# Batch 0 of a fused attention and channel-mix kernel: six loads of k moved to ScalarE's DMA queue and begun ahead

## The chip, the cores and the metric

The kernel runs on one core of a Trainium2 chip. The metric is the device time of one execution in microseconds (us). A profile is one execution with its trace; its span, from the first to the last instruction, is about 1.8 us shorter than the device time of the same execution. Engines: PE is TensorE, DVE is VectorE, ACT is ScalarE, POOL is GpSimd, SP is SyncE, which here only issues DMA. All runs that are compared are fast, apart from one of 743.12 us in the first measurement of the kernel before, which is left out.

## The reference, cut to what matters

```python
def _attn_ref(q, k, v, tau):                       # q, k, v: 4 x 6208 x 256, float32
    qn = q / (norm(q, axis=1) + 1e-06)             # norms over the 6208 rows, one per channel
    kn = k / (norm(k, axis=1) + 1e-06)
    s = kn.transpose(0, 2, 1) @ qn / tau           # 256 x 256 per batch
    a = softmax(s)
    return v @ a
# x = _attn_ref(...); then the channel mix of x: two matmuls with relu squared, gated by a sigmoid
```

For each batch all of q and k must be read before its softmax, and the softmax before the first row of output. For batches 1 to 3 that is hidden behind the mixing of the batch before. For batch 0 nothing can hide it: 12.7 MB (two tensors of 6208 x 256 float32) stand at the start of the kernel.

## The kernel before

Batch 0 is loaded in 14 groups, in the order 1, 2, 0, 3, 4, ... 13. Groups 1 to 11 are 512 rows: one transfer of 512 KB for q and one for k, 128 descriptors of 4 KB each. Group 0 is the 64 left-over rows: 64 descriptors of 1 KB for q, and as many for k. Groups 12 and 13 are half size. Below, "seventh group" means seventh in the order of loading.

```python
    def group_load(b, g):
        rows, n = rows_of(b, g)
        qk = pq.tile([P, S, 2, C], BF16, name="qk", tag="qk", bufs=5)
        groups[b, g] = (qk,)
        if b == 0:
            qk2 = pq.tile([P, S, 2, C], BF16, name="qk2", tag="qk2", bufs=4)
            groups[b, g] += (qk2,)
            t_f = []
            for i, t in enumerate((q, k)):
                f = pq.tile([P, S, C], F32, name=f"f{i}", tag=f"f{i}", bufs=6)
                nc.sync.dma_start(f[:rows, :n], qk_src(t, b, g))
                t_f.append(f)
            groups[b, g] += tuple(t_f)
        # ... (batches 1 to 3 load through GpSimd)

    def group_cast(b, g):
        rows, n = rows_of(b, g)
        qk, qk2, *t_f = groups[b, g]
        for i in range(2):
            nc.vector.tensor_copy(qk[:rows, :n, i, :], t_f[i][:rows, :n])        # to bf16
        for i in range(2):
            nc.scalar.activation(qk2[:rows, :n, i, :], t_f[i][:rows, :n], AF.Square)
    # ...
    nc.scalar.dma_start(mu_rows[0:2], moe_mu_k.rearrange("(h p) -> h p", p=P))   # 1 KB each
    nc.scalar.dma_start(mu_rows[2:4], moe_mu_r.rearrange("(h p) -> h p", p=P))
    # ...
    for g in order(0):
        group_load(0, g)
        group_cast(0, g)
        if g == DIRECT + 1:                     # DIRECT = 9; this is the eleventh group
            copies, gather, roots, evac, invert, turn, exp, weigh = softmax_pieces(0)
            copies()                            # DVE copies the norms' sums out of PSUM
            gather()                            # PE gathers them
        for s in range(sizes(0)[g]):
            unit_matmul(0, g, s)                # s_ps, then PE's sums of the squares (ssq_ps)
        if 5 <= g <= DIRECT:
            keep_warm(3)                        # matmuls that only keep PE busy
    # ... roots, evac, invert, turn (st_ps), exp, weigh: the softmax; then the main pipeline
```

DVE casts, ACT squares, PE multiplies and sums. In the timelines below, ACT's work and the DMA issues of each engine come in the order of the program: in the changed kernel ACT's first square (11.33 us) stands behind its last issue (9.67 us).

## Time and profile before

| kernel before | |
|---|---|
| device time, first measurement | 514.62 and 514.87 us |
| span of the profiled execution | 512.5 us |
| PE busy | 494.6 us (97%) |
| first output-side work (the first `delta` of the mix) | starts at 44.62 us |

The head of the page, its busy rows and its last rows of part 2 (40 slices of 12.8 us; busy share in tenths, then the moved GB/s):

```profile
span 512.5 us, 9496 instructions
PE 494.6 (97%) x3540; PEld 336.7 (66%) x3540; DVE 439.7 (86%) x725; ACT 450.1 (88%) x924; POOL 99.9 (19%) x146
...
PEclk9989999999999999999999999999999999999999
DMA  8999999999989999999599999926498773423123
GB/s 284 410 334 197 198 169 189 148 183 187 207 167 203 185 210 160 163 185 140 96 155 189 186 181 188 186 65 124 83 180 132 114 134 88 101 80 86 44 82 103
```

PE's 97% suggests a kernel that PE bounds, and after the first three slices that is so. But the change touches only those three, and there the moved GB/s are at 410, twice what they are later. The chain that ended last, cut to its longest pieces before 41 us (start, us, what):

```profile
2.18 8.05 DMA f<-in_k_dram
10.26 0.92 ACT qk L144
11.18 9.83 DMA f<-in_k_dram
21.09 10.31 DMA f<-in_k_dram
31.42 0.69 DVE qk L142
32.12 0.61 DVE ssq L225
32.77 1.05 PE bank L232 x8
...
40.37 1.11 PE st_ps L272 x8
```

Until 31.4 us the chain is the loads of q and k. It leaves them at k of the eleventh group (landed at 31.40 us), not at the last group; from there it is PE's work, one piece after the other, to the softmax. The windows view puts the rate of the loads beside it (PE, PEld, DVE, ACT and POOL busy, then the granted clock, the DMA share and GB/s):

```profile
4.00:8.00 4.00, 1.66 (x8) 1.27 (x9) 1.46 (x3) 2.11 (x2) 0.00 (x0) 1.00 0.99 321
8.00:11.00 3.00, 0.99 (x7) 0.21 (x5) 1.44 (x3) 1.80 (x2) 0.00 (x0) 1.00 1.05 283
11.00:31.00 20.00, 17.79 (x113) 8.99 (x113) 10.76 (x17) 16.50 (x18) 0.00 (x0) 1.00 1.02 409
```

From 11 us on the rate is steady at 409 GB/s, one transfer of 512 KB per 1.28 us. From 4 to 11 us it is a quarter lower, though the DMA share says that the engines were occupied (0.99 and 1.05): their packets took longer. SyncE's timeline shows when the loads were issued (start, us it took):

```profile
2.18 0.43 SPq L131 DMA_DIRECT2D f<-in_k_dram  x1
2.65 0.57 SPq L131 DMA_DIRECT2D f<-in_q_dram  x1
3.27 0.59 SPq L131 DMA_DIRECT2D f<-in_k_dram  x1
3.90 0.58 SPq L131 DMA_DIRECT2D f<-in_q_dram  x1
4.52 0.78 SPq L131 DMA_DIRECT2D f<-in_k_dram  x1
5.35 0.65 SPq L131 DMA_DIRECT2D f<-in_q_dram  x1
6.04 0.44 SPq L131 DMA_DIRECT2D f<-in_k_dram  x1
8.18 0.33 SPq L131 DMA_DIRECT2D f<-in_q_dram  x1
10.25 0.33 SPq L131 DMA_DIRECT2D f<-in_k_dram  x1
```

The last two lines are the sixth group. They went out only when the second group's q (8.16 us) and k (10.23 us) had landed: the built program waits so that no more than eight transfers are outstanding.

### The profile page before, as it was taken

The numbers are of one execution on the slowest core, as the hardware profiler recorded it, in microseconds if no ns is written. First come the engines' busy times: TensorE is split into PE (matmuls) and PEld (weight loads), VectorE is DVE, ScalarE is ACT, GpSimd is POOL, SyncE is SP. The second block draws the span as 40 slices with busy tenths as digits, with TensorE's granted clock in tenths as the row PEclk, the third lists the DMA queues.
The fourth block names the chain that finished last, engine by engine and source line by source line (L and its number), as shares of the span: only waits on it lengthen the run. The fifth ranks groups of instructions, "written<-read, shape, count | busy, mean of one in ns | idle before, by whom it ended". The sixth has DMA issues, their size and how long they took to land.

```text
span 512.5 us, 9496 instructions
## 1 busy us (share of the span) xinstructions
PE 494.6 (97%) x3540; PEld 336.7 (66%) x3540; DVE 439.7 (86%) x725; ACT 450.1 (88%) x924; POOL 99.9 (19%) x146
## 2 busy tenths in 40 slices
PE   3889999999999999999999999999999999999996
PEld 1455666776576667667666677677666666666675
DVE  3556899999999999999979999999878787878884
ACT  5886999999899999999899999999887888878784
POOL 0035341223044122121243133000131100000000
PEclk9989999999999999999999999999999999999999
DMA  8999999999989999999599999926498773423123
GB/s 284 410 334 197 198 169 189 148 183 187 207 167 203 185 210 160 163 185 140 96 155 189 186 181 188 186 65 124 83 180 132 114 134 88 101 80 86 44 82 103
DMA packets 133462, 83.46 MB, mean 163 GB/s; under 512 B 50660, under 2 KB 126760, under 8 KB 133416
## 3 DMA queue, kind: packets, MB, share of 16 engines
q0 software_dynamic: 56592, 33.01, 50.0%
q1 hardware_dynamic: 76656, 49.72, 42.9%
q8 instruction: 27, 0.44, 0.3%
q14 instruction: 19, 0.16, 0.1%
q10 hardware_dynamic: 168, 0.13, 0.1%
HBM read 78.71 MB, written 25.43 MB: 203 GB/s over the span
## 4 chain that ended last, share of the span: by engine, by line
PE 85%; DMA 6%; DVE 4%; ACT 4%; issue 1%; SPq 0%; DVEq 0%
PE vr_ps L460 31%; PE kT_ps L423 30%; PE vr_ps L456 8%; PE xT_ps L352 7%; PE s_ps L182 6%; DMA f<-in_k_dram 6%; ACT kr L428 1%; DVE acc L169 1%; DVE xk L408 1%; DVE kk L441 1%; PE st_ps L272 1%; ACT sq L163 1%; ACT xT L354 1%; DVE delta L398 1%; PE junk_ps L513 0%
## 5 line engine op out<-in xcount | busy, mean ns | idle before, releaser
L428 ACT ACTIVATE kr<-kT_ps 128x512 bf16<-128x512 f32 (+1 forms) x392 | 232.7, 605 | 28.9 <-PE kT_ps L423 24.9
L423 PE MATMUL kT_ps<-xk,w_k_sb 128*128 128x512 bf16 (+1 forms) x784 | 231.2, 377 | 0.4 <-DVE xk L408 0.2
L460 PE MATMUL vr_ps<-w_v_sb,kk 128*128 128x256 bf16 x1536 | 231.0, 273 | 0.1
L460 PEld LDWEIGHTS <-kk 128*128 128x128 bf16 x1536 | 149.6, 98 | 58.8 <-DVE kk L441 1.1
L470 DVE SCALAR_TENSOR_TENSOR res<-res,vr_ps 128x256 f32<-128x256 f32 x192 | 79.8, 416 | 44.2 <-ACT res L469 44.1
L441 DVE TENSOR_TENSOR kk<-kr 128x1536 bf16<-128x1536 bf16 (+2 forms) x148 | 116.9, 790 | 0.2 <-ACT kr L428 0.2
L423 PEld LDWEIGHTS <-w_k_sb 128*128 128x128 bf16 x784 | 75.9, 98 | 28.6 <-issue 1.2
L169 DVE TENSOR_TENSOR acc<-acc,sq 128x1024 f32<-128x1024 f32 x69 | 84.0, 1218 | 0.0
L182 PE MATMUL s_ps<-qk 128*128 128x256 bf16 x392 | 73.5, 289 | 6.5 <-DVE qk L142 6.5
L469 ACT ACTIVATE res<-vr_ps 128x256 f32<-128x256 f32 x192 | 76.2, 397 | 1.3 <-PE vr_ps L460 1.3
L456 PE MATMUL vr_ps<-w_r_sb,xr 128*128 128x256 bf16 x384 | 73.3, 272 | 1.2 <-DVE res L470 1.2
L408 DVE SCALAR_TENSOR_TENSOR xk<-delta,mu_t,xT 128x512 bf16<-128x512 bf16 x96 | 71.4, 745 | 0.0
L408 DVE SCALAR_TENSOR_TENSOR xr<-delta,mu_t,xT 128x512 bf16<-128x512 bf16 x96 | 71.3, 745 | 0.0
L456 PEld LDWEIGHTS <-xr 128*128 128x128 bf16 x384 | 37.6, 98 | 46.4 <-issue 2.5
L354 ACT CAST xT<-xT_ps 128x512 bf16<-128x512 f32 x94 | 55.3, 589 | 12.1 <-PE xT_ps L352 12.1
L352 PE MATMUL xT_ps<-vT,a_sb 128*128 128x512 bf16 x188 | 55.9, 379 | 0.2 <-DVE vT L335 0.2
L136 POOL DMA_DIRECT2D qk<-in_q_dram x39 | 26.3, 675 | 143.6 <-ACT kr L428 62.5
L182 PEld LDWEIGHTS <-qk 128*128 128x128 bf16 x392 | 39.4, 103 | 18.1 <-issue 8.1
L165 ACT ACTIVATE sq<-qk 128x1024 f32<-128x1024 bf16 (+1 forms) x49 | 50.8, 1036 | 0.0
L315 POOL DMA_DIRECT2D v_bf<-in_v_dram x48 | 37.4, 782 | 49.6 <-DMA vT<-v_bf 21.3
L398 DVE TENSOR_TENSOR delta<-xT 128x1024 bf16<-128x1024 bf16 x48 | 32.9, 686 | 1.9 <-ACT xT L354 1.8
L144 ACT ACTIVATE qk<-f 128x1024 bf16<-128x1024 f32 (+2 forms) x28 | 26.1, 948 | 8.3 <-DMA f<-in_q_dram 5.3
(82 smaller groups left out, 214.1 us busy)
## 6 DMA issues: line engine op xcount, KB each, us to landing
out_dram<-res SPq DMA_DIRECT2D x47, 512.0 KB, 4.3
v_bf<-in_v_dram POOLq DMA_DIRECT2D x48, 256.0 KB, 9.2
qk<-in_q_dram POOLq DMA_DIRECT2D x36, 256.0 KB, 8.2
qk<-in_k_dram POOLq DMA_DIRECT2D x36, 256.0 KB, 9.2
f<-in_q_dram SPq DMA_DIRECT2D x11, 512.0 KB, 9.0
f<-in_k_dram SPq DMA_DIRECT2D x11, 512.0 KB, 9.9
vT<-v_bf SPq DMA_TRANSPOSE x44, 9.3
f<-in_q_dram SPq DMA_DIRECT2D x2, 256.0 KB, 8.5
```

The costliest lines, as they stand in the source:

```text
L169: nc.vector.tensor_tensor(sums[b], sums[b], t, op=OP.add)
L182: nc.tensor.matmul(s_ps[:, ih, :], rows_at(qk, b, g, 0)[:rows, s, ih * P:(ih + 1) * P], rows_at(qk, b, g, 1)[:rows, s, :], start=t0 and ih ...
L352: nc.tensor.matmul(xT_ps, a_sb[:, b, ih, dh * P:(dh + 1) * P], vT[:, :, ih, :], start=ih == 0, stop=ih == 1)
L354: nc.scalar.copy(xT[:, dh, 1:], xT_ps)
L408: nc.vector.scalar_tensor_tensor(o[:, dh], st[i, "d"][:, dh], mu[:, dh:dh + 1], st[i, "x"][:, dh, :M], op0=OP.mult, op1=OP.add)
L423: nc.tensor.matmul(kT_ps[:, :m], w_k_sb[:, dh, fh * P:(fh + 1) * P], xk[:, dh, :m], start=dh == 0, stop=dh == 1)
L428: nc.scalar.activation(kr, kT_ps[:, :m], AF.Relu, scale=0.5 ** 0.5)
L441: nc.vector.tensor_tensor(st[i, "kk"][:, fh // 4 * 4 + lo:fh + 1, :m], kr, kr, op=OP.mult)
L456: nc.tensor.matmul(vr_ps[:, D:], xr[:, dh, s * P:(s + 1) * P], w_r_sb[:, dh, :], start=dh == 0, stop=dh == 1)
L460: nc.tensor.matmul(vr_ps[:, :D], kk[:, fh, s * P:(s + 1) * P], w_v_sb[:, fh, :], start=fh == 0, stop=fh == 7)
L469: nc.scalar.activation(res[:, s], vr_ps[:, D:], AF.Tanh, scale=0.5)
L470: nc.vector.scalar_tensor_tensor(res[:, s], res[:, s], 1.0, vr_ps[:, :D], op0=OP.add, op1=OP.mult)
```

## The change

The intent is to begin the first six groups at once, k on ScalarE's queue beside q on SyncE's, so that SyncE's issuing doesn't hold back the start. The allocation of the bf16 tiles moves from the load to the cast, so that the loads can stand ahead of everything.

```diff
     def group_load(b, g):
         rows, n = rows_of(b, g)
-        qk = pq.tile([P, S, 2, C], BF16, name="qk", tag="qk", bufs=5)
-        groups[b, g] = (qk,)
         if b == 0:
-            qk2 = pq.tile([P, S, 2, C], BF16, name="qk2", tag="qk2", bufs=4)
-            groups[b, g] += (qk2,)
             t_f = []
             for i, t in enumerate((q, k)):
                 f = pq.tile([P, S, C], F32, name=f"f{i}", tag=f"f{i}", bufs=6)
-                nc.sync.dma_start(f[:rows, :n], qk_src(t, b, g))
+                (nc.scalar if i and order(0).index(g) < 6 else nc.sync).dma_start(f[:rows, :n], qk_src(t, b, g))
                 t_f.append(f)
-            groups[b, g] += tuple(t_f)
+            groups[b, g] = tuple(t_f)
         # ... (batches 1 to 3: the tile is allocated in the else branch)
     def group_cast(b, g):
         rows, n = rows_of(b, g)
-        qk, qk2, *t_f = groups[b, g]
+        t_f = groups[b, g]
+        qk = pq.tile([P, S, 2, C], BF16, name="qk", tag="qk", bufs=5)
+        qk2 = pq.tile([P, S, 2, C], BF16, name="qk2", tag="qk2", bufs=4)
+        groups[b, g] = (qk, qk2)
     # ...
+    for g in order(0)[:6]:
+        group_load(0, g)
     for g in order(0):
-        group_load(0, g)
+        if (0, g) not in groups:
+            group_load(0, g)
         group_cast(0, g)
```

More of the change, by code (lines that the diff above doesn't have):

```diff
@@ L130, in group_load @@
                 f = pq.tile([P, S, C], F32, name=f"f{i}", tag=f"f{i}", bufs=6)
-                nc.sync.dma_start(f[:rows, :n], qk_src(t, b, g))
+                (nc.scalar if i and order(0).index(g) < 6 else nc.sync).dma_start(f[:rows, :n], qk_src(t, b, g))
                 t_f.append(f)
-            groups[b, g] += tuple(t_f)
+            groups[b, g] = tuple(t_f)
         else:
+            qk = pq.tile([P, S, 2, C], BF16, name="qk", tag="qk", bufs=5)
+            groups[b, g] = (qk,)
             for i, t in enumerate((q, k)):
@@ L139, in group_cast @@
         rows, n = rows_of(b, g)
-        qk, qk2, *t_f = groups[b, g]
+        t_f = groups[b, g]
+        qk = pq.tile([P, S, 2, C], BF16, name="qk", tag="qk", bufs=5)
+        qk2 = pq.tile([P, S, 2, C], BF16, name="qk2", tag="qk2", bufs=4)
+        groups[b, g] = (qk, qk2)
         for i in range(2):
```

## The prediction

> **What bounds the kernel now.** The span is 512.5 us; PE is busy 97% of it and makes up 85% of the chain of waits. The change touches only batch 0's q and k, the first 39 us. There the chain is nearly all DMA: "f<-in_k_dram" from 2.18 to 31.42 us, then DVE and PE up to the softmax (st_ps at 40.4 us). The windows view gives 406 to 414 GB/s from 11 to 31 us: transfer-bound, one 512 KB tile per 1.28 us. Before that it is uneven: 407 GB/s at 3 to 4 us, then 254 to 365 GB/s up to 11 us. Against 410 GB/s about 0.75 MB are lost there, an estimated 1.8 us.
>
> The timeline shows why SyncE doesn't issue all at once: an issue takes 0.4 to 0.8 us, and q and k of the sixth group go out only at 8.18 and 10.25 us, as earlier tiles land (at most eight transfers outstanding).
>
> **What the change does.** Six of 28 loads move to ScalarE's queue. Bytes, casts, squares and matmuls are unchanged, as is the built order on PE and DVE. The Trainium skill, "DMA: Bandwidth & Descriptors", section "Issuing engines are not separate DMA queues", says that both queues end on the same 16 DMA engines and only issue time is saved. This trace agrees that issue isn't the limit in the steady part (0.33 us per 1.28 us of transfer). So no higher steady rate; at best part of the 1.8 us comes back.
>
> **What it costs.** In the built order the limit of eight is shared by both queues, and ScalarE executes in order: its six issues stand before its table load (1.28 us) and first square. Its third issue waits for a mu load, the fourth to sixth for landings of q and k of the first group and k of the second. So "all at once" won't happen; the sixth issue goes out when k of the second group lands, which I estimate at 8 to 9.5 us, and the first square starts near 10.2 us instead of 4.12. ScalarE has about 26.4 us of squares (22 at 1.06, four at 0.57, two at 0.4) and took 2.25 of every 2.56 us before: it regains 0.3 to 0.4 us per group. Its backlog of about 4 us should be gone about when the last groups land: squares end at 37 to 38 us (37.3 before). PE's norm matmuls (L197) wait on those squares, so PE idles at 8 to 12 us, then catches up, at half speed until 18 us (8 matmuls 1.87 us, later 1.03). Buffers come free later (seventh q issued at 11.5 us instead of 10.74), but with several tiles still queued; DMA shouldn't starve.
>
> **Sum.** DMA: 0 to -1.5 us. ScalarE/PE backlog at the end of batch 0: 0 to +1. Net about -0.2 us, passed on to the end, because batch 0's softmax gates everything. I predict 514.7 us, 80% range 513.0 to 516.2. Faster by over 2%: 1%; within 2%: 97%; slower: 2%.
>
> **What would show it.** Right: first ACT square at 9 to 11 us; ACT almost without idle from there to 30 us; steady rate near 410 GB/s; last cast of batch 0 at 35 to 37 us; Sqrt within 1.2 us of its 39.08. Wrong: a rate above 420 GB/s, first square before 7 us, or DMA gaps after 11 us because buffers wait for squares.
>
> **What would make it wrong.** The early unevenness may be wholly an effect of the single queue (gain up to 2 us). The late PE may get its full clock one period later than 18 us, or escape or repeat the half-speed stretch at 35 to 38.6 us (about 1 us either way).

## The result, and the profile after

| | before | after |
|---|---|---|
| device time, first comparison | 514.87 us, median of its three fast runs (514.62, 514.87, 516.22) | 513.47 us median (513.42 to 513.62, 4 runs) |
| span of the profiled execution | 512.5 us | 511.8 us |
| Sqrt of the norms starts | 39.08 us | 38.38 us |
| first `delta` starts | 44.62 us | 43.99 us |
| from there to the end | 467.89 us | 467.86 us |

The ratio of the fast runs is 0.9966, with a 95% interval of 0.9945 to 0.9987. A ratio is the mean time of one kernel's fast runs over that of the other's of the same rounds, so it is not quite the ratio of the medians. The change counts as "same" at 2%.

The last two rows say where the difference lies: the part of the kernel after the first `delta` takes the same time in both traces, and the 0.6 to 0.7 us are made before it. The head of the page, its busy row and the GB/s row of its part 2:

```profile
span 511.8 us, 9499 instructions
PE 491.9 (96%) x3540; PEld 336.2 (66%) x3540; DVE 439.6 (86%) x725; ACT 448.2 (88%) x924; POOL 99.9 (20%) x146
...
GB/s 323 409 306 199 196 168 191 163 177 185 214 147 167 204 226 164 162 198 126 101 150 214 151 187 196 181 70 120 83 181 132 97 151 90 100 81 85 43 82 103
```

The traced executions took 514.28 and 513.62 us, 0.66 us apart. The medians are 1.40 us apart, so about half of the timed difference is explained by the traces; the rest belongs to executions that were not traced.

The first slice moves 323 GB/s instead of 284, the second 409 (410 before): the start became faster, the steady rate did not. The same windows of the changed kernel:

```profile
4.00:8.00 4.00, 0.30 (x2) 0.31 (x3) 1.57 (x4) 0.00 (x0) 0.00 (x0) 1.00 1.02 390
8.00:11.00 3.00, 1.80 (x8) 1.03 (x8) 1.61 (x5) 0.96 (x1) 0.00 (x0) 1.00 1.03 355
11.00:31.00 20.00, 16.33 (x118) 8.65 (x117) 10.38 (x17) 19.33 (x23) 0.00 (x0) 1.00 1.03 409
```

ScalarE's timeline of the first 21 us, without its first line, which the prediction was most concerned with:

```profile
1.33 0.24 ACTq L508 DMA_DIRECT2D mu_rows<-in_moe_mu_r_dram  x1
1.60 8.41 ACTq L127 DMA_DIRECT2D f<-in_k_dram  x6
10.04 1.28 ACT L145 ACT_TABLE_LOAD   x1 [10.04 <-DMA f<-in_k_dram]
11.33 10.19 ACT L145 ACTIVATE qk<-f 128x1024 bf16<-128x1024 f32 x12
```

The same two pieces of work in the kernel before:

```profile
1.61 1.28 ACT L144 ACT_TABLE_LOAD   x1 [1.61 <-PEq L696]
4.12 1.06 ACT L144 ACTIVATE qk<-f 128x1024 bf16<-128x1024 f32 x1 [1.23 <-DMA f<-in_q_dram]
```

The loads were not begun at once. ACT's six issues took from 1.60 to 10.01 us, because the last three of them (4.10, 7.19 and 9.67 us) stand until earlier transfers have landed (4.08, 7.17 and 9.65 us). The third waits for a mu load, but that had landed at 2.04 us and cost nothing. The table load and the first square stand behind the issues. The chain of the changed kernel therefore goes through ACT's late start, and leaves it again at 19.65 us (pieces under 0.3 us left out):

```profile
1.99 7.66 DMA f<-in_k_dram
9.67 0.34 ACTq L127
10.04 1.28 ACT L145
...
18.59 1.05 ACT qk L145
19.65 11.13 DMA f<-in_k_dram
30.81 0.69 DVE qk L143
31.50 0.61 DVE ssq L226
32.15 1.05 PE bank L233 x8
...
39.72 1.13 PE st_ps L273 x8
```

From 19.65 us on the chain is one load, from its issue to its landing 11.13 us later. It lay in the queue behind others all that time, while 409 GB/s went on; so the chain's way through ACT up to there doesn't mean that ACT's late start delayed that landing. From k of the eleventh group on the chain is that of the kernel before, 0.6 us sooner at every step (30.78 for 31.40 us, 32.15 for 32.77, 39.72 for 40.37).

In the traces each of these loads ends with 16 reports, one from each DMA engine. So a landing has a middle and a last report, and the work starts after the last: DVE's cast of k of the eleventh group began at 31.42 us, its last report was at 31.40 us. From these records (us):

| landing (last of 16 reports) | before | after | sooner by |
|---|---|---|---|
| k of the first group | 5.80 | 7.17 | -1.37 |
| k of the second group | 10.23 | 9.65 | 0.58 |
| q of the seventh group | 19.74 | 18.01 | 1.73 |
| k of the tenth group | 28.70 | 26.97 | 1.73 |
| q of the eleventh group | 30.11 | 29.50 | 0.61 |
| k of the last group | 36.66 | 36.05 | 0.61 |

Two things happened: 1.73 us were won at the start, and 1.12 us of it were lost between the tenth and the eleventh group. By the middle report 0.99 us were won at q of the seventh group (18.71 to 17.72 us); the rest is a narrower spread between first and last report (1.39 to 0.41 us). The experiments ask what won, and the trace tells what may have lost.

**What lost.** In every trace one packet of 16 KB on the queue that the page calls "instruction" comes between 25.9 and 29.8 us and takes 1.02 to 1.11 us on its engine, against 0.16 us on average for a packet of 4 KB of the loads (11 to 26 us). After the change it starts at 27.02 us and takes 1081 ns; from the transfer then in flight on, the spread between first and last report rises from 0.40 to 1.66 us. Before, it starts at 27.94 us and takes 1079 ns, and the spread rises only from 1.38 to 1.45 us: there five of the 16 reports were 0.6 to 1.0 us behind the middle one already. The middle report of q of the eleventh group was 1.04 us sooner (27.96 against 29.00), the last only 0.61.

Whose instructions are they? In the two traces the packet starts after 221 (before) and 210 (after) PE matmuls and weight loads, and the following ones come at intervals of about 260 of them (484, 749, 991 before). The Trainium skill, "Runtime: NRT & Kernel Launch", section "Instruction fetch mechanics", says that an engine's instructions are refilled in blocks of 16 KiB, 256 instructions, through a DMA queue of the sequencer. That agrees with PE's stream in size and interval. The section calls the cost "mostly hidden", from the side of the engine that is fed. For the loads, which share a DMA engine with the block, it doesn't look hidden here. That the packet causes the lag is read from the coincidence in 13 of the 14 traces (in two of them, before and one_queue, the spread rose by 0.2 us or less), not from a run that moves the packet alone. (In the fourteenth, late_act, the spread was 2.05 us before and after.)

### The profile page after: what moved, and what is told of

Same layout as the page of the kernel before. It is cut to its first block, busy times and chain, and to the rows that moved or that the text cites. A ratio compares the mean times of both kernels' runs of the same rounds, so it can differ in the third digit from the quotient of the medians.

```text
span 511.8 us, 9499 instructions
## 1 busy us (share of the span) xinstructions
PE 491.9 (96%) x3540; PEld 336.2 (66%) x3540; DVE 439.6 (86%) x725; ACT 448.2 (88%) x924; POOL 99.9 (20%) x146
## 4 chain that ended last, share of the span: by engine, by line
PE 86%; ACT 5%; DVE 4%; DMA 4%; issue 1%; ACTq 0%; DVEq 0%
PE vr_ps L461 31%; PE kT_ps L424 30%; PE vr_ps L457 8%; PE xT_ps L353 7%; PE s_ps L183 7%; DMA f<-in_k_dram 4%; ACT kr L429 1%; DVE acc L170 1%; DVE xk L409 1%; DVE kk L442 1%; ACT qk L145 1%; PE st_ps L273 1%; ACT sq L164 1%; ACT xT L355 1%; DVE delta L399 1%
## 5 line engine op out<-in xcount | busy, mean ns | idle before, releaser
L183 PE MATMUL s_ps<-qk 128*128 128x256 bf16 x392 | 71.8, 283 | 3.7 <-DVE qk L143 3.7
L143 DVE CAST qk<-f 128x1024 bf16<-128x1024 f32 (+2 forms) x28 | 17.5, 644 | 14.0 <-DMA f<-in_k_dram 9.4
```

What stands on the lines that cost most here:

```text
L183: nc.tensor.matmul(s_ps[:, ih, :], rows_at(qk, b, g, 0)[:rows, s, ih * P:(ih + 1) * P], rows_at(qk, b, g, 1)[:rows, s, :], start=t0 and ih ...
```

## The experiments

Twelve runs were made, in three groups, each group on one chip and on another chip than the last. A comparison of two times is made only within a group.

**Group 1: is it the queue?** The first trace alone doesn't even show that the slow start belongs to the kernel. So the kernel before was traced again.

before_again: no edit.

> The kernel before, unchanged, profiled a second time. The first trace of it shows three stalls of the loads: eight packets of 0.75 to 1.5 us at 4.6 to 4.9 us, and all packets slowed to 0.3 to 0.5 us at 8.0 to 9.0 and 9.5 to 10.3 us. Theory A (the single queue causes the slow start): they come again, about 250 to 370 GB/s from 4 to 11 us, and k of the sixth group lands near 18.5 us again. Rival B (chance, a disturbance of that one execution): the second trace has other or no stalls, 390 to 410 GB/s from 3 us on, and k of the sixth group lands near 16.5 to 17 us. Ratio to before: 1.000 within 0.003 in both.

Measured: the slow start came again: 323 GB/s from 4 to 8 us and 299 from 8 to 11 us, nine packets over 0.6 us (up to 1.61 us) near 4.6 to 6.0 us. Theory A holds against chance. The time is a warning, though: 513.79 us median (513.60 to 514.30), ratio 0.9973 (0.9957 to 0.9990) to the identical kernel before, whose 11 runs on the same chip lay between 513.56 and 515.93 us. Two identical programs differ by as much as the change gains, with an interval that leaves 1 out. So the time of one pair of programs proves nothing under half a per cent, and the traces have to carry the argument.

one_queue: the change, with all loads on SyncE's queue.

```diff
-                (nc.scalar if i and order(0).index(g) < 6 else nc.sync).dma_start(f[:rows, :n], qk_src(t, b, g))
+                nc.sync.dma_start(f[:rows, :n], qk_src(t, b, g))
```

> The change with all loads on SyncE's queue: only the order of buffer allocation and the up-front loop are left of it. Theory A (the second queue gives the gain): as before, 250 to 370 GB/s from 4 to 11 us, q of the seventh group lands near 19.7 us, ratio 1.000 within 0.001. Rival C (the order of allocation gives it): ratio 0.997, early rate near 390 GB/s.

Measured: 345 and 310 GB/s in the two windows, three packets of 1.37 to 1.48 us at 4.97 to 5.02 us, q of the seventh group at 19.70 us; ratio 1.0002 (0.9986 to 1.0019). The allocation and the loop ahead do nothing that shows; rival C falls. (This trace also has five packets of 0.62 to 0.99 us near 1.8 to 2.5 us. Such early ones come with one queue and with two, in late_act, shallow, after and two_in_order as well, and are not counted here.)

late_act: one_queue, and ACT must first copy one element of the second group's k.

```diff
     for g in order(0)[:6]:
         group_load(0, g)
+    held = const.tile([P, 1], F32, name="held")
+    nc.scalar.copy(held, groups[0, order(0)[1]][1][:, 0, 0:1])
```

> All loads on SyncE's queue, as one_queue, but ScalarE copies one element of the second group's k before its first square, so that its squares start as late as in the changed kernel (about 10 us). Rival D (the early stalls come from ScalarE's table load and squares running beside the first loads, and the change gains by holding ScalarE back): early rate near 390 GB/s, q of the seventh group lands near 18 us, ratio near 0.997. Theory A (queue): early rate as before, 19.7 us, ratio 1.000 to 1.004, because the late squares are then on top of the late loads.

Measured: 347 and 326 GB/s, one packet of 1.30 us at 4.80 us, q of the seventh group at 19.83 us; ratio 0.9993 (0.9977 to 1.0010). The first square began at 10.32 us. So holding ACT back doesn't make the loads faster; rival D falls. It also bounds the price of the late squares: against one_queue, k of the last group landed at the same time (36.51 and 36.52 us), Sqrt came 0.25 us later (39.09 against 38.84), and the matmuls after it (st_ps) only 0.03 us later (40.22 against 40.19). Even the 0.25 us need not be the squares': in both traces the chain from k of the eleventh group on is PE's, and PE's half-clock stretch began 0.42 us sooner in late_act (33.71 against 34.13 us).

two_on_act: only k of the first two groups on ACT's queue, which no landing holds up.

```diff
-                (nc.scalar if i and order(0).index(g) < 6 else nc.sync).dma_start(f[:rows, :n], qk_src(t, b, g))
+                (nc.scalar if i and order(0).index(g) < 2 else nc.sync).dma_start(f[:rows, :n], qk_src(t, b, g))
```

> Only k of the first two groups on ScalarE's queue, which no landing holds up, so that ScalarE's squares start near 4 us as before. Theory A: the early rate is 390 GB/s or more as in the change, q of the seventh group lands near 18 us and ratio 0.995 to 0.998. Rival D (late ScalarE helps): stalls are back, ratio near 1.000. If the queue must stay shared for all six groups, the rate falls back after the second group.

Measured: 371 and 393 GB/s, no packet over 0.6 us before 26 us, q of the seventh group at 17.89 us, first square at 4.02 us; 513.60 us median (513.41 to 513.75), ratio 0.9968 (0.9954 to 0.9983). In these traces two transfers on the second queue bring all that six bring, and ACT isn't held up. Span and Sqrt are as after the change (511.8 us, 38.30 us), which agrees with late squares that cost next to nothing.

**Group 2: what is the slow start made of?** All traces with one queue have two dips: long packets at 4.6 to 5 us, and a general slowness at 8 to 10.5 us, when the 1 KB packets of group 0 pass.

late_left: the kernel before, with group 0 loaded seventh.

```diff
-        return [1, 2, 0] + g[3:]
+        return [1, 2, 3, 4, 5, 6, 0] + g[7:] if b == 0 else [1, 2, 0] + g[3:]
```

> The kernel before (one queue), with the short group 0 (64 rows of 1 KB for q and for k) loaded seventh instead of third. All four traces with one queue have two stalls: single packets of 0.65 to 1.6 us at 4.6 to 5.0 us, and 190 to 290 GB/s at 8 to 10.5 us. Theory E (the second stall belongs to the 1 KB packets of group 0, which pass at 7.5 to 9.5 us): the first stall stays, 8 to 10.5 us runs at 380 GB/s or more, and a smaller dip comes where group 0 now passes (near 16 to 18 us). Rival F (it belongs to the number of transfers issued at the start to one queue): both stalls stay where they were. Time within 0.3% of before in both cases.

Measured: 338 GB/s from 4 to 8 us, with six packets of 0.93 to 1.51 us, but 412 from 8 to 11 us; the spread of the landings rose from 1.15 to 2.12 us where group 0 now passed, near 18 to 21 us. So the second dip belongs to group 0 (theory E), the first doesn't. Time 514.42 us, ratio 0.9989 (0.9970 to 1.0008): the dip is moved, not removed.

shallow: the kernel before, with fewer transfers outstanding at the start.

```diff
                 f = pq.tile([P, S, C], F32, name=f"f{i}", tag=f"f{i}", bufs=6)
+                if 3 <= order(0).index(g) < 6:
+                    nc.vector.memset(f[:, 0, 0:1], 0.0)
 # ... and in the main loop the load of the group three places ahead stands behind the cast
```

> The kernel before (one queue, same order), but the loads of the fourth to sixth group each wait until an earlier group is cast (a one-column write to their buffers), so that at 4.5 us only three large and two small transfers are outstanding on the queue instead of five large and two small. Theory F (issuing many transfers into one queue at the start stalls it): no single packets over 0.6 us near 4.6 to 5.0 us, 380 GB/s or more from 4 to 7 us, and issues of 0.3 to 0.5 us. Rival E (the kind of transfer): the first stall goes or stays by chance, the second stays at 8 to 10.5 us. If neither changes, both fall.

Measured: with nothing issued between 3.85 and 6.34 us there still were four packets of 0.99 to 1.17 us at 4.79 to 4.86 us, and 302 GB/s at 8 to 11 us. So the first dip comes without many issued transfers and without SyncE's issuing at that moment; theory F falls as it was put. The rate from 4 to 8 us was 371 GB/s, though, above the other traces with one queue (321 to 347), so that a deep queue makes the dip worse isn't excluded. (The hold was too long: the fifth group went out at 10.40 us, and the rate was 205 GB/s from 11.5 to 12.0 us. The time, 515.61 us, ratio 1.0016 with 0.9988 to 1.0044, is of no use for that reason.)

two_late_left: two_on_act, with group 0 loaded seventh, the same edit as in late_left.

> k of the first two groups on ScalarE's queue and group 0 loaded seventh. Theory E: the remaining dip of two_on_act (336 to 358 GB/s at 6 to 9 us, where the 1 KB packets passed) goes or moves to near 16 us; q of the eighth group in order lands 0.3 us or more sooner than in two_on_act by the sum of bytes; the time is 0 to 0.4 us under two_on_act (513.6 us). Rival F: no change, 513.6 us.

Measured: 408 GB/s from 4 to 8 us and 419 from 8 to 11 us. The two edits together remove both dips:

| GB/s at 4 to 8 / 8 to 11 us | one queue | two queues |
|---|---|---|
| group 0 third | 321 / 283 (before) | 371 / 393 (two_on_act) |
| group 0 seventh | 338 / 412 (late_left) | 408 / 419 (two_late_left) |

The windows of the two kernels on the diagonal:

```profile
4.00:8.00 4.00, 2.15 (x13) 1.37 (x13) 1.60 (x4) 2.26 (x3) 0.00 (x0) 1.00 1.02 338
8.00:11.00 3.00, 1.59 (x10) 0.88 (x7) 1.81 (x3) 2.53 (x3) 0.00 (x0) 1.00 1.01 412
```

(late_left, above: the first window slow, the second not.)

```profile
4.00:8.00 4.00, 0.23 (x1) 0.28 (x2) 1.50 (x4) 1.80 (x2) 0.00 (x0) 1.00 1.03 371
8.00:11.00 3.00, 2.99 (x16) 1.59 (x16) 2.12 (x5) 2.83 (x5) 0.00 (x0) 1.00 1.02 393
```

(two_on_act: in the first window group 0's small packets pass, and they cost less than with one queue.) And yet the time did not follow: 514.66 us (513.79 to 515.58), ratio 0.9994 (0.9976 to 1.0011). q of the eighth group, up to which all orders have moved the same bytes, landed at 20.30 us against 20.44 in two_on_act, not the 0.3 us sooner that were expected: group 0 slows the loads wherever it passes. The last group landed at 35.71 against 35.78. And PE's clock was halved for 6.83 us (30.41 to 37.23) instead of 3.41, and Sqrt came at 39.17 us instead of 38.30: by the chain, the eight matmuls of the gather took 1.86 us instead of 1.05. (The Trainium skill, "TensorE: Matmul & The Clock Gate", section "Part 1: The HAM clock gate", gives windows of 3413 ns, after an idle one of which the clock is halved. The stretches of 3.41 and 6.83 us agree with the length. The idle window isn't there: in the 3.41 us before this stretch PE was busy 46% of the time, and its longest gap was 1.86 us.) In this trace faster loads at the start were worth nothing at the softmax, because PE was at half clock when they had landed.

two_early_gather: two_on_act, with the copy and gather of the norms before the eleventh group's cast.

```diff
-        group_cast(0, g)
         if g == DIRECT + 1:
             copies, gather, roots, evac, invert, turn, exp, weigh = softmax_pieces(0)
             copies()
             gather()
+        group_cast(0, g)
```

> two_on_act with the copy and the gather of the squared norms placed before the casts of the eleventh group instead of after them. In the changed kernel PE runs without a pause from the gather at 32.15 us to Sqrt at 38.38 us, and the gather waits for a copy that stands behind the cast of the eleventh group's k, while its data was there at 29.8 us. If that chain sets the end of batch 0: gather near 30.6 us, Sqrt 0.5 to 1.5 us sooner than 38.4 us, time 512.3 to 513.1 us. If the last landings set it instead: Sqrt within 0.3 us of 38.4 us and 513.6 us.

Measured: a miss. Sqrt came at 38.66 us, time 513.73 us (513.41 to 514.19), ratio 0.9975 (0.9960 to 0.9990), no better than two_on_act. By these numbers the second alternative would hold, but the chain does not go through the last landings: it leaves the loads at k of the tenth group and is PE's from there. PE's clock was halved from 30.17 to 37.00 us, so the eight matmuls of the gather took 1.71 us instead of 1.05, and the eight of the eleventh group 1.87 us. It waited idle for the tenth group's k until 28.84 us; that load was in flight when the 16 KB packet came (last report 28.07 us, middle 26.43).

**Group 3: order or queue, and PE's clock.** With two queues the transfers are also served in another order (q, q, k, q of group 0, k, ...). That had to be told apart. This chip was noisier: the kernel before scattered over 514.42 to 519.29 us, and no time of this group tells kernels apart. The traces do.

order_only: all on SyncE's queue, issued in the order in which the two queues had been served.

```diff
+    for i, at in ((0, 0), (0, 1), (1, 0), (0, 2), (1, 1), (0, 3), (1, 2), (0, 4), (1, 3), (0, 5), (1, 4), (1, 5)):
+        g = order(0)[at]
+        rows, n = rows_of(0, g)
+        nc.sync.dma_start(groups[0, g][i][:rows, :n], qk_src((q, k)[i], 0, g))
```

> All loads on SyncE's queue, but issued in the order in which the changed kernel's two queues were served: q, q, k of the first two groups, then q of group 0, k of the second, and so on. Theory A (two queues remove the first stall): packets of 0.65 to 1.6 us come again at 4.6 to 5.0 us, 240 to 320 GB/s at 4.5 to 6 us. Rival G (the order in which q and k follow each other removes it): no packet over 0.6 us before 26 us, 380 GB/s or more at 4 to 6 us. Time 514 to 516 us under A, 513.4 to 513.8 us under G.

Measured: five packets of 0.64 to 1.12 us at 4.67 to 4.92 us, 346 and 348 GB/s: the first dip is there, in its old place. The order alone doesn't remove it; rival G falls. But the order isn't without effect: from 8 to 11 us the rate was 348 GB/s, against 283 to 326 in the traces with one queue and the old order, and q of the eighth group landed at 21.60 us, against 22.07 to 22.39 in all others with one queue. Time 515.98 us, ratio 1.0017 (0.9975 to 1.0059).

two_in_order: k of the first two groups on ACT's queue with the mu loads behind them, so that q and k begin in the old order.

```diff
-    for g in order(0)[:6]:
+    for g in order(0)[:2]:
+        group_load(0, g)
+    nc.scalar.dma_start(mu_rows[0:2], moe_mu_k.rearrange("(h p) -> h p", p=P))
+    nc.scalar.dma_start(mu_rows[2:4], moe_mu_r.rearrange("(h p) -> h p", p=P))
+    for g in order(0)[2:6]:
         group_load(0, g)
 # ... the two mu loads are taken out above, and mu's transpose stands behind the seventh group
```

> k of the first two groups on ScalarE's queue, with the small mu loads moved behind them, so that the transfers begin in the order of the kernel before: q, k, q, k, group 0. Theory A: no packet over 0.6 us before 26 us, 380 GB/s or more at 4 to 6 us; rival G: the long packets at 4.6 to 5.0 us are back. The dip of group 0 (330 to 360 GB/s near 6 to 9 us) is there in both.

Measured: no long packet at 4.6 to 5 us and 407 GB/s from 4 to 8 us, but four packets of 0.61 to 0.67 us at 2.9 us (221 GB/s from 3.0 to 3.5 us), and group 0 cost more than in two_on_act (302 GB/s from 8 to 11 us). It lands q of the eighth group at 21.25 us. So theory A is right about the place, and wrong in saying that two queues have no stall at all: both queues began at 0.74 us here, and the stall came early and short. And with the old order, two queues gave only part of the gain (21.25 us, against 20.57 after the change). How the gain divides between queue and order can't be said from single traces on this chip.

two_warm: two_on_act with seven filling matmuls after the tenth group and six after the ninth.

```diff
-            keep_warm(3)
+            keep_warm(7 if g == DIRECT else 6 if g == DIRECT - 1 else 3)
```

> two_on_act with seven filling matmuls instead of three after the tenth group and six after the ninth, in time in which PE waited for loads. In all traces but one PE runs at half clock for 3.41 or 6.83 us between 30 and 40 us, where its work on the last groups is the chain to the softmax. If idle PE before that is the cause and the half-speed work is on the chain: no half-clock stretch there, Sqrt at 37.7 to 38.0 us instead of 38.30, time 513.0 to 513.3 us. If not: 513.6 us or, if the filling matmuls themselves hold up the chain, 514 us or more.

Measured: in its trace Sqrt came at 37.83 us, within the expected 37.7 to 38.0, the span was 511.3 us, and PE kept its full clock. The windows view of 30 to 38 us, two_on_act first:

```profile
30.00:38.00 8.00, 6.10 (x76) 5.08 (x77) 4.73 (x9) 7.08 (x9) 5.34 (x9) 0.79 1.00 264
```

```profile
30.00:38.00 8.00, 7.89 (x102) 5.96 (x103) 4.81 (x9) 7.33 (x11) 5.25 (x9) 1.00 1.01 267
```

The granted clock, the third figure from the right, is 0.79 and 1.00. By time it is unclear: 516.17 us (513.42 to 520.52), ratio 1.0019 (0.9972 to 1.0066). And full clock there came without filling too, in before_again and after_again. So two_warm is the best trace, not a proven best kernel.

after_again: the changed kernel, no edit.

> The changed kernel once more. No packet over 0.6 us before 26 us, q of the seventh group lands at 17.9 to 18.1 us, time 513.4 to 513.7 us in all executions, while those of the kernel before scatter over 513.6 to 516.4 us.

Measured: 515.92 us (514.47 to 518.02), ratio 1.0000 (0.9967 to 1.0032): on this chip no gain can be seen, and the changed kernel's own time scattered. No packet over 0.6 us at the start, as expected, and 369 GB/s from 4 to 11 us. But from the second transfer on one report in 16 came late: q of the second group had its middle report at 5.12 us and its last at 6.93 (5.18 and 5.40 in the first trace). One or more engines stayed behind (at k of the tenth group four reports of 16 were 0.7 us or more behind the middle one; three packets of 0.70 to 1.02 us had come between 17.2 and 20.1 us), with the 16 KB packet the spread went from 1.47 to 3.01 us, and k of the last group landed at 37.53 us. Why they fell behind in this execution isn't known; two_warm, on the same chip, has 5.09 and 5.31.

All traces together, sorted by the landing of q of the eighth group:

| kernel | queues | q of eighth group, us | last landing, us | Sqrt, us | span, us |
|---|---|---|---|---|---|
| two_early_gather | 2 | 20.21 | 35.73 | 38.66 | 512.4 |
| two_late_left | 2 | 20.30 | 35.71 | 39.17 | 512.5 |
| two_on_act | 2 | 20.44 | 35.78 | 38.30 | 511.8 |
| two_warm | 2 | 20.45 | 35.87 | 37.83 | 511.3 |
| after | 2 | 20.57 | 36.05 | 38.38 | 511.8 |
| two_in_order | 2 | 21.25 | 37.01 | 39.39 | 512.9 |
| order_only | 1 | 21.60 | 36.41 | 38.94 | 519.7 |
| after_again | 2 | 21.81 | 37.53 | 39.49 | 513.4 |
| shallow | 1 | 22.07 | 37.14 | 41.06 | 514.4 |
| before_again | 1 | 22.09 | 36.68 | 38.64 | 512.5 |
| late_left | 1 | 22.14 | 37.47 | 39.89 | 513.3 |
| one_queue | 1 | 22.26 | 36.52 | 38.84 | 512.9 |
| before | 1 | 22.30 | 36.66 | 39.08 | 512.5 |
| late_act | 1 | 22.39 | 36.51 | 39.09 | 513.6 |

Sqrt isn't yet the outcome. before_again kept full clock and had Sqrt 0.44 us sooner than before, but began the next matmuls (st_ps) at 40.36 us against 40.35: there the chain went from k of the twelfth group (34.02 us) through ACT's last squares instead of PE.

(order_only lost about 7 us after 44 us, outside the part that this change touches; with 0.83 granted clock from 100 to 120 us it isn't a start effect.)

## Why the prediction was right or wrong

The measured 513.47 us lies in the range of 513.0 to 516.2 us, and "within 2%" came true. That alone says little: the range also holds every time of the unchanged kernel in group 1 (513.56 to 515.93 us), so a change that did nothing would have hit it too. Point by point:

- **The bound was right.** Batch 0's start is bound by the transfers. The steady rate did not change: 409 GB/s from 11 to 31 us in both. The Trainium skill, "DMA: Bandwidth & Descriptors", section "Issuing engines are not separate DMA queues", says that queues of several engines end on the same DMA engines and save only issue time. The steady part agrees. The start doesn't quite: with the same bytes, the change raised 4 to 11 us from 304 to 375 GB/s. The new order on one queue (order_only) had 347 there, the old order on two queues (two_in_order) 362.
- **"At best part of the 1.8 us comes back" was right.** By the middle report 0.99 us had come back by the seventh group, by the last report 1.73. At the end 0.61 us were left; the rest was lost when the 16 KB packet came, which the prediction did not see. The term of the sum, "0 to -1.5 us", holds the 0.61. That it does is in part luck: the prediction reckoned with the mean rate, not with single engines that lag behind.
- **"All at once won't happen" was right.** The sixth issue came at 9.67 us (predicted 8 to 9.5) and the first square at 11.33 us (near 10.2, in a band of 9 to 11): 0.17 and 0.33 us outside the bands.
- **The backlog cost nothing.** Predicted 0 to +1 us. ACT worked almost without idle from 11.33 to 29.1 us and had caught up at 29.60 us, where it waited for the eleventh group's load. From 19.65 us on no square is on the chain. late_act bounds the price: 0.25 us at Sqrt, 0.03 us after it.
- **The net of -0.2 us was too small.** In the two first traces it is -0.70 us at Sqrt, -0.63 us at the first `delta` and -0.7 us in the span. In the timed runs it was -0.3% in the first comparison and none to be seen on the chip of group 3, and an identical kernel differed by 0.27%. What the change is worth in general is not settled: the two intervals reach from 2.8 us gained (0.9945) to 1.7 us lost (1.0032). With two queues q of the eighth group landed sooner in six traces of seven than in any with one (after_again is the exception); at the last landing two_in_order and after_again, both on the last chip, were later than most.
- **PE's clock was named as a risk, and moved.** The full clock came at 16.45 us instead of 18.10, and the half-speed stretch at 33.52 to 36.93 us instead of 35.17 to 38.58. It lay on the chain in both traces, so its cost cancels in their difference; that is luck. In the second trace of the changed kernel (after_again) and of the kernel before (before_again) it was absent, and in three other kernels it was doubled (6.83 us).

What stays open: why a single queue stalls about when its third transfer is moved. It isn't chance (seven traces of seven), and it came without the old allocation, without ACT's work beside it, with fewer transfers issued, and in another order of q and k. It goes with the queue, and in two_in_order a shorter stall came at 2.9 us. No run here shows what in the path of a queue causes it, and none moves the 16 KB packet alone.

## What to carry to other kernels

When a stage is bound by loads, look at the report of every DMA engine, not only at the mean rate: here what waited, waited for the last of 16 reports, and the lead that 15 of them kept was lost to one that fell 1.26 us behind. Putting two early transfers on a second queue can smooth the start of a burst without raising its steady rate, but ACT, given more issues than may be outstanding, stood from 1.60 to 10.01 us with all its own work behind them. Before believing a gain of a third of a per cent, run the unchanged kernel against itself.

## What the Trainium skill lacked or had wrong

- "DMA: Bandwidth & Descriptors", section "Issuing engines are not separate DMA queues", says that issuing from several engines saves only issue time. Here the loads ran at 321 to 347 GB/s from 4 to 8 us in six of seven traces with one queue (371 in shallow), and at 367 to 408 in seven with two, though the small packets of group 0 fell into that window too in most of those. The page has nothing of a stall at the start of a burst (packets of 0.6 to 1.6 us instead of about 0.16 us).
- "Runtime: NRT & Kernel Launch", section "Instruction fetch mechanics", calls the cost of a 16 KiB block mostly hidden, and has nothing of what it does to other transfers on the same DMA engine. A block of that size took 1.02 to 1.11 us on one DMA engine in all 14 traces, and when it came in the changed kernel, the spread of the loads' reports rose by 1.26 us (0.40 to 1.66), to the end of the loading.
- "DMA: Bandwidth & Descriptors" has no figure for mixing a small transfer into a stream: the 128 KB of group 0 (64 rows of 1 KB, twice) went with a dip to 283 GB/s over 3 us with one queue in the old order (348 in order_only), and cost little less when it came later.
- "TensorE: Matmul & The Clock Gate", section "Part 1: The HAM clock gate", has the clock halved after an idle window of about 3.4 us. In the 11 traces with a half-clock stretch after 30 us, PE was busy 37 to 76% of the 3.41 us before it, and no gap there was longer than 2.14 us.
